# The last 50 microseconds of a Fourier mixer beside softmax attention: eight weight loads earlier on SyncE, two VectorE instructions further back, and two small jobs given to VectorE

## The chip, the cores and the metric

One core of a Trainium2 chip runs the whole program. The metric is device time in microseconds (us), of one execution from start to end. Three runs of the kernel before gave a median of 1685.47 us (1683.25 to 1685.73).

## The reference

Two mixers read the same 2048 x 512 input `x`, and a gate per row blends them:

```python
a = einsum("bsd,ed->bse", x, dft_hid_re); b = einsum("bsd,ed->bse", x, dft_hid_im)
y = einsum("ts,bse->bte", dft_seq_re, a) - einsum("ts,bse->bte", dft_seq_im, b)
...
qkv = x @ wqkv                                   # 32 heads of 16 columns
p = softmax(q @ k.T * 16 ** -0.5)                # 2048 x 2048 for each head
attn = (p @ v) @ wo
...
g = sigmoid((x * gate_w).sum(-1))
out = g * y + (1 - g) * attn
```

## The kernel before

**Tiles.** TensorE (PE) multiplies in fp32r, and where precision matters a value is split in a rounded part "hi" and a rest "lo" (`hi_lo`, line 84: hi by ScalarE, lo by VectorE; `parts`, line 574: both by VectorE). A product is then hi x hi + hi x lo + lo x hi, three matmuls into one PSUM bank. PSUM has eight banks of 128 x 512; a small planner (`bank`, line 384) hands them out in the order in which it believes they come free.

**Heads and units.** The heads run in 16 pairs. The work of a pair is cut into 32 units, 512 in all; a unit is four score tiles (matmul L738, exponential on ScalarE L739 into a tile `pt`). A tile of row maxima is a matmul L223 and a reduction on VectorE (DVE) L225. The values of two units are one group of 16 matmuls in the profile (L774, for the last pair L755).

**Sections.** The program is a written-out stream of sections. A section holds eight score tiles and, mixed in between, other matmuls: first the Fourier part, and near the end the output projection (`proj`, L429: matmuls of attention output by `wo_hl`, three or nine for a row tile of 128 rows). At a section's end come, in this order, the steps of a table `plan` that are due (`at(u, step)`: the step is issued at the end of the section whose first unit is u or u - 1), then a function of its own for some sections (`after`, line 992), then the values of two units. Each engine executes its instructions in the order in which they were issued.

**The last block.** Attention output is stored to HBM, divided by its softmax sums there, and read back as the stationary operand of `proj`. For the last heads of the first 1024 rows this goes as follows. SyncE (SP) stores `osum` (L792) and reads the sums into `rc` (L528, unit 498). DVE takes reciprocals (L534, unit 500), SP stores them to `r` (L539) and loads outputs and reciprocals into `o_raw` (L552, L553: `last_block` step 0). GpSimd (POOL) multiplies the two (L587, step 1, unit 503). DVE rounds the product into `o_l`, hi by L575 and lo by L576 (step 2, unit 505). The `proj` matmuls that read `o_l` begin with the section behind it.

**The last pair.** The last pair's 1024 late rows are done in two blocks of eight units and without HBM (`LastPair`): `copy` moves the sums of the values out of PSUM (L666), `turn` brings them to rows on PE (L672), takes reciprocals (L674) and scales (L676), `back` transposes on PE (L682) and splits into `o15` (L85, L86), and `products` multiplies by `w15` (L691). For block 0 these steps hang between the sections of units 502 to 511, for block 1 they come after the last section (`last_pair`, line 701). `w15` is a rearranged piece of `wo` that eight DMAs load (`load_w15`, L649, unit 504) into the memory that `osum` held.

**The row tiles.** `finish` (line 602) adds a projected tile to the output rows `yp`: either in one DVE instruction (L609), or, for the tiles in `by_others`, by ScalarE (ACT) into `few` (L606) and POOL (L607). Then SP stores the rows (L627, L697).

## Time and profile before

| what | value |
|---|---|
| median of three runs | 1685.47 us |
| the profiled execution: its own time, its span | 1684.99 us, 1683.2 us |
| PE busy, its granted clock | 99% of the span, 0.999 |
| DVE, ACT, POOL busy | 82%, 74%, 45% |
| PE in the chain that ended last | 97% |
| DVE, POOL, DMA in that chain | 1% each |

The span runs from the first instruction to the last; 1.8 us lie around it. PE is busy nearly all the time, so time can only be lost or won where PE stands still, or behind its last matmul. All that the change touches lies in the last 50 us of the span.

### The profile page before, as it was taken

The page shows a single profiled execution, that of the slowest core. Times are in us where ns is not written, and L with a number is a line of the kernel's source. Part 1 is how long each engine was busy: PE and PEld are TensorE (multiplying, and loading weights), DVE is VectorE, ACT ScalarE, POOL GpSimd, SP SyncE. Part 2 cuts the span into 40 slices and gives each one's busy share as a digit, 9 for nine tenths or more (in the row PEclk, how much of TensorE's full clock was granted, in tenths as well). Part 3 has the DMA queues.
Part 4 walks back from the last instruction along what each step waited for, and adds up shares of the span by engine and source line. Part 5 has one row for each costly group of instructions (what it writes and reads, how often), then busy time and mean ns, then how long its engine had stood idle before and what let it go on. Part 6 is the DMA issues. An engine that isn't in the chain of part 4 may idle for free.

```text
span 1683.2 us, 34607 instructions
## 1 busy us (share of the span) xinstructions
PE 1670.9 (99%) x13120; PEld 1014.2 (60%) x13120; DVE 1376.7 (82%) x2295; ACT 1246.9 (74%) x2471; POOL 751.0 (45%) x814
## 2 busy tenths in 40 slices
PE   9999999999999999999999999999999999999997
PEld 7888766655555555555555555555555555555554
DVE  5448688888888888888888888888888888888875
ACT  5212288887777888778777787777777888888885
POOL 0214634544444466445444566454544455422241
PEclk9999999999999999999999999999999999999999
DMA  9973500314141432414165533423241535730114
GB/s 289 344 156 107 177 13 14 52 46 82 45 83 46 88 103 84 77 46 92 39 141 190 103 117 83 93 58 70 70 87 41 103 102 125 275 66 15 34 27 139
DMA packets 82622, 165.16 MB, mean 98 GB/s; under 512 B 19904, under 2 KB 20168, under 8 KB 78616
## 3 DMA queue, kind: packets, MB, share of 16 engines
q1 hardware_dynamic: 77832, 162.30, 37.4%
q8 instruction: 103, 1.69, 0.5%
q0 software_dynamic: 4480, 0.39, 0.3%
q14 instruction: 63, 0.52, 0.1%
q10 hardware_dynamic: 144, 0.26, 0.0%
HBM read 107.73 MB, written 54.52 MB: 96 GB/s over the span
## 4 chain that ended last, share of the span: by engine, by line
PE 97%; DVE 1%; POOL 1%; DMA 1%; issue 0%; SPq 0%; ACT 0%; DVEq 0%; POOLq 0%; ACTq 0%
PE d L429 39%; PE t L774 27%; PE t L223 11%; PE t L738 7%; PE t L318 4%; PE t L89 2%; PE t L90 2%; PE t L91 2%; PE t L336 1%; PE t L755 1%; PE t L429 0%; DVE mx L225 0%; DMA o_raw<-r 0%; PE t L160 0%; POOL hl L295 0%
## 5 line engine op out<-in xcount | busy, mean ns | idle before, releaser
L225 DVE TENSOR_REDUCE mx<-t 128x1 f32<-128x512 f32 x2022 | 1255.5, 684 | 211.1 <-PE t L223 160.4
L739 ACT ACTIVATE pt<-t 128x512 f32<-128x512 f32 x2048 | 1034.5, 629 | 12.4 <-PE t L738 12.2
L738 PE MATMUL t<-qs,ks 50*128 50x512 f32 x2048 | 741.3, 409 | 3.1 <-DVE on L676 2.3
L223 PE MATMUL t<-ks,qs 48*128 48x512 f32 x2022 | 690.1, 400 | 0.1
L429 PE MATMUL d<-xab,ch 64*128 64x512 f32 x2016 | 657.5, 401 | 0.0
L774 PE MATMUL t<-pt,vt 128*32 128x512 f32 x3968 | 477.2, 598 | 0.2
L429 PEld LDWEIGHTS d<-xab,ch 64*128 64x128 f32 x2016 | 357.8, 184 | 130.9 <-issue 98.9
L223 PEld LDWEIGHTS t<-ks,qs 48*128 48x128 f32 x2022 | 367.7, 185 | 82.5 <-ACT pt L739 41.1
L738 PEld LDWEIGHTS t<-qs,ks 50*128 50x128 f32 x2048 | 370.4, 185 | 72.9 <-DVE mx L225 38.6
L429 PE MATMUL d<-xab,cl 64*128 64x512 f32 x1008 | 403.4, 400 | 0.0
L789 POOL TENSOR_TENSOR osum<-osum,oe 128x512 f32<-128x512 f32 x217 | 279.4, 1287 | 161.6 <-ACT oe L783 159.0
L783 ACT COPY oe<-t 128x512 f32<-128x512 f32 x217 | 127.5, 588 | 231.3 <-PE t L774 229.2
L774 PEld LDWEIGHTS t<-pt,vt 128*32 128x32 f32 x3968 | 103.9, 109 | 231.2 <-issue 148.4
L374 POOL CAST ch<-craw 128x512 fp32r<-128x512 f32 x126 | 77.2, 612 | 351.5 <-PE t L738 281.1
L429 PEld LDWEIGHTS d<-xab,cl 64*128 64x128 f32 x1008 | 185.8, 184 | 67.4 <-issue 50.3
L375 POOL TENSOR_TENSOR cl<-craw,ch 128x512 fp32r<-128x512 f32 x126 | 162.3, 1288 | 10.2
L248 POOL DMA_DIRECT2D qs<-mt x132 | 74.1, 567 | 78.8 <-DVE mt L244 73.8
L429 PE MATMUL d<-wo_hl,o_hl 64*128 64x512 f32 x288 | 77.3, 395 | 0.0
L429 PE MATMUL d<-wre,xab 64*128 64x512 f32 x288 | 70.5, 389 | 0.0
L429 PEld LDWEIGHTS d<-wo_hl,o_hl 64*128 64x128 f32 x288 | 52.2, 185 | 13.6 <-DVE yp L609 5.0
L429 PEld LDWEIGHTS d<-wre,xab 64*128 64x128 f32 x288 | 52.9, 185 | 3.8 <-DVE mx L225 0.3
L89 PE MATMUL t<-xab,wh 128*128 128x512 f32 x128 | 50.4, 394 | 0.0
(121 smaller groups left out, 914.0 us busy)
## 6 DMA issues: line engine op xcount, KB each, us to landing
craw<-w_seq SPq DMA_DIRECT2D x128, 256.0 KB
qk<-hl SPq DMA_DIRECT2D x32, 512.0 KB
qs<-qk SPq DMA_DIRECT2D x96, 128.0 KB
ks<-qk SPq DMA_DIRECT2D x96, 128.0 KB
b<-hl SPq DMA_DIRECT2D x16, 512.0 KB
xab<-b SPq DMA_DIRECT2D x16, 512.0 KB
o<-osum SPq DMA_DIRECT2D x62, 128.0 KB
oh<-nh SPq DMA_DIRECT2D x12, 512.0 KB
```

The source lines that it names most:

```text
L89: nc.tensor.matmul(ps, sh, mh, start=first, stop=False)
L223: nc.tensor.matmul(ps, qs[p % 2][r, qt * P:(qt + 1) * P], ks[p % 2][r, kb * 512:(kb + 1) * 512], start=True, stop=True)
L225: user = nc.vector.tensor_reduce(mx[p % 2][:, h, qt, kb:kb + 1], ps, AX.X, ALU.max)
L248: (nc.sync, nc.gpsimd)[h].dma_start(rows.rearrange("v (q b c) -> v b q c", q=n, b=4)[:, b], mt[k % 2][32 * b + h:32 * b + 4 * n:2])
L374: nc.gpsimd.tensor_copy(h1, raw)
L375: nc.gpsimd.tensor_tensor(l1, raw, h1.bitcast(F32), ALU.subtract)
L429: i = nc.tensor.matmul(self.ps, st[r], mv[r], start=not self.begun, stop=stop)
L738: nc.tensor.matmul(ps, ks[p % 2][rr, kt * P:(kt + 1) * P], qs[p % 2][rr, q0:q0 + 512], start=True, stop=True)
L739: return nc.scalar.activation(pts[u][:, 2 * qb + h], ps, AF.Exp, bias=0.0, scale=DH ** -0.5)
L774: nc.tensor.matmul(acc[32 * j:32 * j + 32], vt[:, kt, p, h:h + 32], pt[:, j], start=u == us[0], stop=u == us[-1])
L783: nc.scalar.copy(oe, acc)
L789: nc.gpsimd.tensor_tensor(o, o, oe, ALU.add)
```

## The change

```diff
@@ LastPair.back
-            hi_lo(self.o15[:, 0], self.o15[:, 1], t[:, :P])
+            if self.blk:
+                parts(self.o15[:, 0], self.o15[:, 1], t[:, :P])
+            else:
+                hi_lo(self.o15[:, 0], self.o15[:, 1], t[:, :P])
@@ last_pair
-        by_others.update((5, 6))
+        by_others.add(6)
@@ the plan
-    for step, u in enumerate((500, 503, 505)):
+    for step, u in enumerate((500, 503, 507)):
         at(u, last_block, step, 0, 4, nc.gpsimd)
-    at(504, load_w15)
+    at(499, load_w15)
```

Lines behind 683 stand three lines further down in the kernel of the change (L738 is L741 there, L649 stays).

**The rounding.** On DVE, at the end of the sections of units 504 and 506; the number behind a name is a buffer's. Before:

```order
L609 SCALAR_TENSOR_TENSOR yp15_20723<-d_23280,omg_166,yp15_20723 128x512
L575 CAST o_l_23304<-o_raw_22715 128x1024
L576 TENSOR_TENSOR o_l_23304<-o_raw_22715,o_l_23304 128x1024
L674 RECIPROCAL rc15_23075<-t_23307 128x8
L676 TENSOR_TENSOR on15_23074<-t_23307,rc15_23075 128x4x16 x2
L609 SCALAR_TENSOR_TENSOR yp13_20658<-t_23328,omg_166,yp13_20658 128x512
L609 SCALAR_TENSOR_TENSOR yp14_20722<-t_23342,omg_166,yp14_20722 128x512
L609 SCALAR_TENSOR_TENSOR yp15_20723<-d_23354,omg_166,yp15_20723 128x512
L86 TENSOR_TENSOR o15_23076<-t_23369,o15_23076 128x128
```

And now:

```order
L609 SCALAR_TENSOR_TENSOR yp15_20723<-d_23289,omg_166,yp15_20723 128x512
L674 RECIPROCAL rc15_23075<-t_23304 128x8
L676 TENSOR_TENSOR on15_23074<-t_23304,rc15_23075 128x4x16 x2
L609 SCALAR_TENSOR_TENSOR yp13_20658<-t_23325,omg_166,yp13_20658 128x512
L609 SCALAR_TENSOR_TENSOR yp14_20722<-t_23339,omg_166,yp14_20722 128x512
L609 SCALAR_TENSOR_TENSOR yp15_20723<-d_23351,omg_166,yp15_20723 128x512
L575 CAST o_l_23366<-o_raw_22715 128x1024
L576 TENSOR_TENSOR o_l_23366<-o_raw_22715,o_l_23366 128x1024
L86 TENSOR_TENSOR o15_23076<-t_23369,o15_23076 128x128
```

The two instructions that write `o_l` stood ahead of block 0's reciprocals and now stand one section later, behind three row tiles and ahead of block 0's `o15`.

**The loads.** On SP, from the last store of `osum` on. Before:

```order
L792 DMA o_104<-osum 64x512 x2
L528 DMA rc<-o_104 64x1x64 x2
L248 DMA qs_935<-mt_174 2x4x32 x4
L539 DMA r_151<-rc 16x4x64 x2
L552 DMA o_raw<-o_104 64x1x1024
L553 DMA o_raw<-r_151 64x1x1024
L552 DMA o_raw<-o_104 64x1x1024
L553 DMA o_raw<-r_151 64x1x1024
L649 DMA w_23295<-wo_141 16x1024 x8
L627 DMA out<-yp_21644 128x512
```

And now:

```order
L795 DMA o_104<-osum 64x512 x2
L528 DMA rc<-o_104 64x1x64 x2
L649 DMA w_23127<-wo_141 16x1024 x8
L248 DMA qs_935<-mt_174 2x4x32 x4
L539 DMA r_151<-rc 16x4x64 x2
L552 DMA o_raw<-o_104 64x1x1024
L553 DMA o_raw<-r_151 64x1x1024
L552 DMA o_raw<-o_104 64x1x1024
L553 DMA o_raw<-r_151 64x1x1024
L627 DMA out<-yp_21644 128x512
```

The eight loads of `w15` stood last and now pass the rows of maxima that the scores of the last eight units need (`qs<-mt`), the store of the reciprocals and the four loads of `o_raw`.

**The end.** On DVE, the row tiles 4, 5 and 7 with block 1 of the last pair between them. Before:

```order
L609 SCALAR_TENSOR_TENSOR yp_qs0_22513<-t_23485,omg_166,yp_qs0_22513 128x512
L674 RECIPROCAL rc15_23318<-t_23511 128x8
L676 TENSOR_TENSOR on15_23317<-t_23511,rc15_23318 128x4x16 x2
L86 TENSOR_TENSOR o15_23319<-t_23526,o15_23319 128x128
L609 SCALAR_TENSOR_TENSOR yp_qs0_22513<-t_23530,omg_166,yp_qs0_22513 128x512
```

And now:

```order
L609 SCALAR_TENSOR_TENSOR yp_qs0_22513<-t_23485,omg_166,yp_qs0_22513 128x512
L609 SCALAR_TENSOR_TENSOR yp_qs0_22513<-t_23504,omg_166,yp_qs0_22513 128x512
L674 RECIPROCAL rc15_23315<-t_23510 128x8
L676 TENSOR_TENSOR on15_23314<-t_23510,rc15_23315 128x4x16 x2
L575 CAST o15_23316<-t_23525 128x128
L576 TENSOR_TENSOR o15_23316<-t_23525,o15_23316 128x128
L609 SCALAR_TENSOR_TENSOR yp_qs0_22513<-t_23529,omg_166,yp_qs0_22513 128x512
```

Row tile 5 is one more L609 on DVE and one L606 and one L607 fewer on ACT and POOL; block 1's hi, L85 on ACT before, is L575 on DVE. PE's instructions stand in the same order before and now.

## The prediction

> **What bounds the kernel now.** PE is busy for 99% of the span, so I looked first for the place in the last 55 us where it is not. The waits of PE there name a single one (us in total, times, longest):

> ```profile
> PE t L738 <- DVE on L676: 2.3, 1, 2.3
> ```

> The chain of work that ended last, in order of time, shows how DVE came to be late (start, duration, what):

> ```profile
> 1652.44 2.38 POOL o_raw L587
> ...
> 1654.85 0.70 DVE o_l L575
> ...
> 1655.58 1.23 DVE o_l L576
> ...
> 1656.95 0.37 DVE on L676 x2
> ...
> 1657.45 0.47 PE t L738
> ```

> The reader is to see a detour. PE needs the PSUM bank that L676 reads, so it waits for L676. But L676 has nothing to do with `o_raw`: it stands in DVE's queue behind L575 and L576, and these wait for POOL's product. The timeline of DVE gives its last work ahead of that wait, and the first and the last of the three row tiles behind L676:

> ```profile
> 1651.13 0.75 DVE L609 SCALAR_TENSOR_TENSOR yp<-d,omg,yp 128x512 f32<-128x512 f32 x1
> 1657.22 0.74 DVE L609 SCALAR_TENSOR_TENSOR yp<-t,omg,yp 128x512 f32<-128x512 f32 x1
> 1658.92 0.75 DVE L609 SCALAR_TENSOR_TENSOR yp<-d,omg,yp 128x512 f32<-128x512 f32 x1
> ```

> The timeline of PE gives an undisturbed section (from 1648.73 to L672), the disturbed one (from 1653.98 to the transpose L682) and the first reader of `o_l`:

> ```profile
> 1648.73 0.50 PE L738 MATMUL t<-qs,ks 50*128 50x512 f32 x1
> 1651.10 1.10 PE L672 MATMUL t<-pairsum,oe 128*128 128x64 f32 x8
> 1653.98 0.50 PE L429 MATMUL t<-wo_hl,o_lnh 64*128 64x512 f32 x1
> 1654.56 0.39 PE L429 MATMUL t<-wo_hl,o_lnh 64*128 64x512 f32 x1
> 1654.79 0.39 PE L429 MATMUL t<-wo_hl,o_lnh 64*128 64x512 f32 x1
> 1657.45 0.47 PE L738 MATMUL t<-qs,ks 50*128 50x512 f32 x1 [2.27 <-DVE on L676]
> 1659.04 0.33 PE L682 MATMUL t<-ident,on 128*128 128x128 f32 x1
> 1661.15 0.49 PE L429 MATMUL t<-wo_hl,o_l 64*128 64x512 f32 x1
> ```

> **The rounding moved back.** The sums that the reciprocals read are finished when L672 ends, at 1651.10 + 1.10 = 1652.20; DVE has been idle since 1651.13 + 0.75 = 1651.88. With L575 and L576 gone from its front, the reciprocal and L676 run at once. Between the end of L576 (1655.58 + 1.23 = 1656.81) and that of L676 (1656.95 + 0.37 = 1657.32) lie 0.5, so they end near 1652.8. PE's matmuls follow each other at 0.23 (1654.79 - 1654.56), so it asks for the bank at 1655.02, when it has been free for 2.2. The matmul of 1657.45 runs **2.43 earlier**.

> What is late next? First the transpose L682, which waited for row tiles. The undisturbed section took 2.37 from its first matmul to L672 (1651.10 - 1648.73); from 1653.98 that makes 1656.35. The second row tile of the section reads the two L429 behind the bank, which start at 1655.0 to 1655.3 and end by 1655.7; with its 0.75, one such tile ahead of it on DVE, it is through at 1656.5. So the transpose comes at 1656.5 to 1656.7 where it was at 1659.04: the gain is still 2.3 to 2.5. Then `o_l`, which now stands behind the third row tile. That tile ended at 1658.92 + 0.75 = 1659.67 and moves with PE to 1657.25. L575 adds 0.70, L576 1.23, the gaps 0.05: hi at 1658.0, lo at 1659.25. The first reader of hi moves from 1661.15 to about 1658.7. The third matmul of that row tile, the first reader of lo, stands 0.58 behind (1654.56 - 1653.98), at 1659.3. So hi has 0.7 of slack and lo hardly any; I take no wait, and keep up to 0.5 of loss for the range. POOL's product, ready at 1654.82, has 2.4 to spare. `o15` of block 0 (L86) now follows L576; its reader, L691, comes a full section later.

> The term: **-2.4 us** (-1.9 to -2.6).

> **The eight loads moved forward.** SP's DMA queue in the timeline (start, duration of the group):

> ```profile
> 1634.84 1.21 SPq L528 DMA_DIRECT2D rc<-o  x2
> 1639.78 2.73 SPq L248 DMA_DIRECT2D qs<-mt  x4
> 1643.55 1.21 SPq L539 DMA_DIRECT2D r<-rc  x2
> 1647.34 5.26 SPq L649 DMA_DIRECT2D w<-wo  x8
> ```

> And what SP waited for:

> ```profile
> SPq L248 <- DVE mt L244: 3.6, 1, 3.6
> SPq L649 <- DMA o_raw<-r: 1.3, 1, 1.3
> SPq L649 <- DMA o_raw<-o: 0.5, 1, 0.5
> ```

> The 5.26 hold 1.8 of waiting for loads of `o_raw` that stood ahead; without it the eight take 3.46, 0.43 each. The neighbours L528 and L539 take 0.6 each (1.21 for two), the dearest that I would assume: 4.8 for eight. In the new place they start at 1634.84 + 1.21 = 1636.05 behind transfers that are small or done, and end at 1639.5 to 1640.9. SP stood idle there for 3.6, waiting for the row maxima, so `qs<-mt` moves by 0 to 1.1. Who waits for it? The fifth score of a section, in the timeline of PE:

> ```profile
> 1645.47 0.49 PE L738 MATMUL t<-qs,ks 50*128 50x512 f32 x1
> ```

> The only landing that the trace gives for these transfers is that of POOL's four:

> ```profile
> DMA to landing us min/median/max: 1.6/1.7/3.4
> ```

> The last of SP's four went out a quarter of 2.73 ahead of the group's end, at 1641.8, and landed by that near 1643.5: 2.0 ahead of its reader, 0.3 at the longest landing. A shift of 1.1 leaves 0.9, or costs 0.8; I take 0, since 0.43 is this very transfer's price. The store of the reciprocals keeps its time, as it waits for DVE until 1643.55. The loads of `o_raw` lose their company and may land sooner; once the rounding has moved, nobody waits for that. Term: **0** (0 to +0.8).

> [...]

> **The end of the program.** Tile 5's matmuls are the first row of PE's timeline here; tile 7's are the third, and the last is the product with `o15`:

> ```profile
> 1672.18 0.98 PE L429 MATMUL t<-wo_hl,o_l 128*128 128x512 f32 x3
> 1674.69 0.33 PE L682 MATMUL t<-ident,on 128*128 128x128 f32 x1
> 1674.78 0.94 PE L429 MATMUL t<-wo_hl,o_l 128*128 128x512 f32 x3
> 1675.69 0.97 PE L691 MATMUL t<-w,o 32*128 32x512 f32 x12
> ```

> DVE ahead of the reciprocal, and ACT:

> ```profile
> 1674.04 0.21 DVE L674 RECIPROCAL rc<-t 128x8 f32<-128x8 f32 x1 [1.37 <-PE t L672]
> ```

> ```profile
> 1674.79 0.69 ACT L606 ACTIVATE few<-d,omg 128x512 f32<-128x512 f32 x1 [0.85 <-PE d L429]
> 1675.37 0.26 ACT L85 CAST o<-t 128x128 fp32r<-128x128 f32 x1
> ```

> Tile 5 is ready for DVE at 1672.18 + 0.98 = 1673.16, and DVE is idle for 1.37 ahead of the reciprocal; an L609 (0.74) ends at 1673.9, before 1674.04: free. Block 1's hi waited on ACT behind tile 6. Rounding 128 x 128 from PSUM on DVE is not in the trace; between a reciprocal of 8 columns (0.21) and a row tile of 512 (0.74), I take 0.26, what ACT needs. The transpose ends at 1675.02, so hi is there at 1675.35 instead of 1675.63. But PE has tile 7 to do until the third matmul has started near 1675.33, so L691 starts at 1675.56 at best, 0.13 sooner. Does the end follow? The DMA engines in windows (last columns: busy share, GB/s):

> ```profile
> 1677.00:1677.40 0.40, 0.00 (x0) 1.00 0.00 0
> 1677.40:1681.60 4.20, 1.27 (x1) 0.86 0.97 373
> ```

> 4.2 us at 373 GB/s are 1.57 MB, the last six stored tiles (tiles 6, 7 and block 1's four, 128 x 512 x 4 bytes each), without a gap. The train starts with tile 6, which keeps its way over ACT and POOL. Tile 5 was out of its way before, since the engines stood at 0 ahead of it. Term: **0** (-0.4, if the end follows the chain instead, to +0.1).

> **Sum.** -2.4 against the profiled execution's 1684.99 is 1682.6 (span 1680.8). That execution lies 0.48 below the median of the runs; from the median it is 1683.1, which I give: 0.14% less.

> **The rivals.**
> - *The wait becomes one for `o_l`.* If the row tiles run later than drawn, PE waits at the first reader of lo, one for one. For it: lo has no slack. Against it: hi has 0.7 and POOL 2.4. With a whole L576 lost, 1.2: 1684.3.
> - *The loads hold up SP: slower.* If they wait in the new place as two of them did in the old, they push `qs<-mt`. The gain is gone when that shift reaches 2.0 + 2.4 = 4.4, that is when the eight take 3.6 + 4.4 = 8.0, or 1.0 each. At 1.2 each the shift is 6.0 and the score waits 4.0: 1685.47 - 2.4 + 4.0 = 1687.1. Against it: what they waited for then is not ahead of them now. [...]
> - *The bank was not what PE waited for.* The releaser is inferred. If it was another, nothing is won: 1685.4. Against it: L676 ended at 1657.32, and PE started 0.13 later.
> - *More than forecast.* The end follows the chain by 0.4: -2.8, 1682.7.

> **How the numbers follow.** Forecast 0.68, `o_l` 0.12, SP 0.08 (half of it slower than before), bank 0.04, more 0.08. A measurement of this kernel can tell about 0.2%, 3.4 us, from no change, and no case reaches that by itself on the fast side. But the three runs lie 2.5 us apart, so a median can be a microsecond off: a fifth of the forecast and half of "more" fall beyond, 0.18. Slower: half of the SP case and a little of the bank, 0.06. Within: 0.76. The range takes the forecast with "more" and the scatter below it (1680.9), and `o_l` and the bank above (1685.7).

> **What would show it.** Right: no L676 in the waits of PE; the L575 of `o_l` directly behind an L609 and not behind POOL; the first matmul of `o_l` 2.3 to 2.5 sooner, counted from the first of the section before; `qs<-mt` no later than 1.1 behind its old distance from L244. Wrong: a wait of PE for L576, or for a DMA at the fifth score behind L248; a train of stores that starts over 0.3 sooner behind the last values.

## The result and the profile after

The changed kernel takes **1681.95 us** (median of 20 executions, 1681.30 to 1682.79), the kernel before beside it 1685.50 (20 executions, 1683.25 to 1688.00). The ratio is 0.9981, with a 95% interval of 0.9975 to 0.9987: 0.19% less, 3.2 to 3.6 us. Two things are to be explained. The gain is about 1 us larger than the forecast, and the executions of the kernel before lie 4.75 us apart, those of the changed one 1.5. Between the two profiled executions the gain is only 1684.99 - 1682.39 = 2.60.

The waits of PE in the last 55 us of the changed kernel are an empty list. The timeline of PE has the section that was disturbed before (start, duration; from L429 at 1653.80 to the transpose L682) and the first matmuls that read `o_l`:

```profile
1650.91 1.10 PE L672 MATMUL t<-pairsum,oe 128*128 128x64 f32 x8
...
1653.80 0.50 PE L429 MATMUL t<-wo_hl,o_lnh 64*128 64x512 f32 x1
...
1654.38 0.62 PE L741 MATMUL t<-qs,ks 50*128 50x512 f32 x2
...
1656.42 0.33 PE L682 MATMUL t<-ident,on 128*128 128x128 f32 x1
1656.68 1.92 PE L758 MATMUL t<-pt,vt 128*32 128x512 f32 x16
1658.54 0.49 PE L429 MATMUL t<-wo_hl,o_l 64*128 64x512 f32 x1
...
1659.11 0.39 PE L429 MATMUL t<-wo_hl,o_l 64*128 64x512 f32 x1
```

From the section's first matmul to the first reader of `o_l` it took 7.17 before (1661.15 - 1653.98) and takes 4.74 now: 2.43 less. The rest of the 2.60 between the profiles is 0.18 that lay upstream of the section already (1653.98 against 1653.80). DVE in the same stretch:

```profile
1652.05 0.21 DVE L674 RECIPROCAL rc<-t 128x8 f32<-128x8 f32 x1 [0.35 <-PE t L672]
1652.29 0.36 DVE L676 TENSOR_TENSOR on<-t,rc 128x64 f32<-128x64 f32 x2
1654.80 1.45 DVE L609 SCALAR_TENSOR_TENSOR yp<-t,omg,yp 128x512 f32<-128x512 f32 x2 [2.15 <-PE t L429]
1656.31 0.75 DVE L609 SCALAR_TENSOR_TENSOR yp<-d,omg,yp 128x512 f32<-128x512 f32 x1
1656.98 0.68 DVE L575 CAST o_l<-o_raw 128x1024 fp32r<-128x1024 f32 x1
1657.69 1.22 DVE L576 TENSOR_TENSOR o_l<-o_raw,o_l 128x1024 fp32r<-128x1024 f32 x1
```

The reader is to see three things. The reciprocal waits for PE alone. L676 is through at 1652.65, so the bank is free long before PE asks for it (1654.61, the second of the two scores from 1654.38). And L576 ends at 1658.91, 0.20 ahead of its first reader at 1659.11. SP's queue and POOL's product:

```profile
1634.66 1.21 SPq L528 DMA_DIRECT2D rc<-o  x2
1635.92 3.83 SPq L649 DMA_DIRECT2D w<-wo  x8
1639.85 2.74 SPq L248 DMA_DIRECT2D qs<-mt  x4
```

```profile
1651.74 2.37 POOL L587 TENSOR_TENSOR o_raw<-o_raw 128x1024 f32<-128x1024 f32 x1 [9.67 <-DMA o_raw<-r]
```

The eight loads take 0.48 each and fill what was SP's wait for the row maxima. The fifth score starts 1.19 behind its section's first matmul, as before (1645.29 - 1644.10; 1645.47 - 1644.28). POOL's product starts 0.5 sooner beside the upstream 0.18; whether that is because the loads of `o_raw` have no weights beside them is not shown (see the eight loads alone). The end, from PE, from DVE (block 1's hi) and in windows around the train of the last stores (last two columns: DMA share, GB/s):

```profile
1673.02 0.97 PE L694 MATMUL t<-w,o 32*128 32x512 f32 x12
```

```profile
1672.43 0.29 DVE L575 CAST o<-t 128x128 fp32r<-128x128 f32 x1 [0.42 <-PE t L682]
```

```profile
1674.70:1675.10 0.40, 0.00 (x0) 0.00 (x0) 0.40 (x2) 0.00 (x0) 0.32 (x1) 1.00 0.00 0
1675.10:1679.00 3.90, 0.00 (x0) 0.00 (x0) 1.01 (x2) 0.00 (x0) 0.94 (x1) 0.71 1.04 402
```

From the last product to the end of the span it is 7.58 (1680.6 - 1673.02), before 7.51 (1683.2 - 1675.69). The end has given nothing.

### The profile page after: what moved, and what is told of

Its sections match the earlier page's. It is cut to its first block, busy times and chain, and to the rows that moved or that the text cites. A ratio compares the mean times of both kernels' runs of the same rounds, so it can differ in the third digit from the quotient of the medians.

```text
span 1680.6 us, 34603 instructions
## 1 busy us (share of the span) xinstructions
PE 1670.8 (99%) x13120; PEld 1016.6 (60%) x13120; DVE 1378.1 (82%) x2297; ACT 1245.8 (74%) x2469; POOL 750.9 (45%) x813
## 4 chain that ended last, share of the span: by engine, by line
PE 98%; POOL 1%; DVE 1%; issue 0%; DMA 0%; SPq 0%; ACT 0%; DVEq 0%; POOLq 0%; ACTq 0%
PE d L429 40%; PE t L777 27%; PE t L223 11%; PE t L741 7%; PE t L318 4%; PE t L90 2%; PE t L89 2%; PE t L91 2%; PE t L336 1%; PE t L758 1%; PE t L429 1%; DVE mx L225 0%; PE d L223 0%; PE t L160 0%; POOL hl L295 0%
## 5 line engine op out<-in xcount | busy, mean ns | idle before, releaser
L741 PE MATMUL t<-qs,ks 50*128 50x512 f32 x2048 | 741.6, 409 | 0.8 <-ACT y L445 0.5
L429 PE MATMUL d<-xab,ch 64*128 64x512 f32 x2016 | 657.5, 401 | 0.0
L429 PEld LDWEIGHTS d<-xab,ch 64*128 64x128 f32 x2016 | 357.7, 184 | 132.9 <-issue 98.9
L741 PEld LDWEIGHTS t<-qs,ks 50*128 50x128 f32 x2048 | 370.4, 185 | 67.1 <-DVE mx L225 37.9
L429 PE MATMUL d<-xab,cl 64*128 64x512 f32 x1008 | 403.6, 400 | 0.0
L429 PEld LDWEIGHTS d<-xab,cl 64*128 64x128 f32 x1008 | 185.7, 184 | 67.8 <-issue 51.1
L248 POOL DMA_DIRECT2D qs<-mt x132 | 74.3, 568 | 77.7 <-DVE mt L244 72.6
L429 PE MATMUL d<-wo_hl,o_hl 64*128 64x512 f32 x288 | 77.3, 395 | 0.0
L429 PE MATMUL d<-wre,xab 64*128 64x512 f32 x288 | 70.4, 389 | 0.0
L429 PEld LDWEIGHTS d<-wo_hl,o_hl 64*128 64x128 f32 x288 | 52.2, 185 | 13.4 <-DVE yp L609 5.0
L429 PEld LDWEIGHTS d<-wre,xab 64*128 64x128 f32 x288 | 52.9, 185 | 3.9 <-DVE mx L225 0.3
```

What stands on the lines that cost most here:

```text
L248: (nc.sync, nc.gpsimd)[h].dma_start(rows.rearrange("v (q b c) -> v b q c", q=n, b=4)[:, b], mt[k % 2][32 * b + h:32 * b + 4 * n:2])
L429: i = nc.tensor.matmul(self.ps, st[r], mv[r], start=not self.begun, stop=stop)
L741: nc.tensor.matmul(ps, ks[p % 2][rr, kt * P:(kt + 1) * P], qs[p % 2][rr, q0:q0 + 512], start=True, stop=True)
```

## The experiments

Four theories stood against each other. **W**: all of the gain is PE's one wait on L676, and that wait is longer or shorter from run to run. **L**: what the medians have beyond it comes from the weights, which no longer load beside `o_raw`. **E**: it comes from the end. **C**, formed after the first four runs: PE's idle time lets its granted clock fall in a part of the executions. Each kernel below ran against the kernel before on the same chip; intervals are 95%.

### The rounding alone

```diff
 kernel before
-    for step, u in enumerate((500, 503, 505)):
+    for step, u in enumerate((500, 503, 507)):
```

> The kernel before with the rounding of the last block one section later and nothing else (507 for 505). Theory W (all of the gain is PE's one wait, and its length varies from run to run with the landing of o_raw, so its mean is larger than the profiled 2.27): the whole gain comes here, a median near 1682.0 and runs that lie within 2 us of each other, as those of the change do; no wait of PE on L676. Theory L (what goes beyond the forecast 2.4 comes from the weights no longer loading beside o_raw): 1683.1 here. Theory E (it comes from the end of the program): 1683.1 here too.

Measured: 1681.63 (1681.29 to 1682.15, 11 runs), ratio 0.9978 (0.9969 to 0.9987). That is the whole gain, and the spread is gone with it. PE waits for nothing in the last 50 us of its profile. L and E fall as causes of the rest.

### The eight loads alone

```diff
 kernel before
-    at(504, load_w15)
+    at(499, load_w15)
```

> The kernel before with the eight weight loads moved forward and nothing else (499 for 504). Theory W: o_raw lands 0.5 to 0.7 sooner than in the profile of before, PE's wait on L676 is still there and shorter by that, 1684.5 to 1685.0, and the runs still spread over 3 us or more. Theory L: about 1684.4, and the spread becomes small, as the weights were what disturbed the landing. Theory E: as before less the 0.5 at most.

Measured: 1685.13 (1683.11 to 1686.70, 11 runs), ratio 0.9996 (0.9987 to 1.0005): no difference. Its profile shows something new. The timeline of PE, and four slices of 0.25 us (third column from the end: the granted clock):

```profile
1655.94 0.47 PE L738 MATMUL t<-qs,ks 50*128 50x512 f32 x1 [1.78 <-DVE on L676]
...
1657.87 3.47 PE L755 MATMUL t<-pt,vt 128*32 128x512 f32 x16
```

```profile
1657.25:1657.50 0.25, 0.12 (x2) 0.00 (x0) 0.25 (x2) 0.25 (x2) 0.00 (x0) 1.00 0.00 0
1657.50:1657.75 0.25, 0.24 (x1) 0.14 (x1) 0.25 (x1) 0.25 (x2) 0.00 (x0) 0.72 0.00 0
...
1660.75:1661.00 0.25, 0.25 (x4) 0.00 (x0) 0.00 (x0) 0.00 (x0) 0.00 (x0) 0.50 0.00 0
1661.00:1661.25 0.25, 0.25 (x4) 0.00 (x0) 0.00 (x0) 0.00 (x0) 0.00 (x0) 0.96 0.00 0
```

The wait is 0.5 shorter than before (1.78), since POOL's product comes sooner: 0.86 behind the start of L672 (1650.93 - 1650.07) against 1.34 before (1652.44 - 1651.10). That the new place of the loads does this is not shown, as the product comes just as soon, 0.88 behind (1650.56 - 1649.68), in the kernel with PE kept busy, where the loads stand in their old place. But 1.7 us after PE is back at work its clock goes to a half, and stays there for 3.4 us. The 16 value matmuls take 3.47 where they took 1.92: 1.55 lost, behind the wait. That the wait is the cause is theory C, which comes from this run.

### The end alone

```diff
 kernel before
-            hi_lo(self.o15[:, 0], self.o15[:, 1], t[:, :P])
+            if self.blk:
+                parts(self.o15[:, 0], self.o15[:, 1], t[:, :P])
+            else:
+                hi_lo(self.o15[:, 0], self.o15[:, 1], t[:, :P])
...
-        by_others.update((5, 6))
+        by_others.add(6)
```

> The kernel before with the two edits at the end and nothing else (both parts of block 1's rounding and tile 5 on VectorE). Theory W and L: nothing, within 0.2 of before (1685.3 to 1685.7), with the spread of before; the train of stores at the end starts at the same distance behind the last value group. Theory E: 1684.4, and the train starts about 1 us sooner.

Measured: 1685.37 (1683.37 to 1687.21, 11 runs), ratio 0.9999 (0.9990 to 1.0008). These edits are worth nothing, and the spread is that of before.

### Tile 6 on DVE as well

```diff
 changed kernel
-        by_others.add(6)
```

> The kernel of the change with row tile 6 on VectorE too, so that only block 1's first tile still goes over ScalarE and GpSimd. If the end is a train of six stores that starts with tile 6 (as the prediction has it), the train starts 1 to 1.3 us sooner and the end comes 0.3 to 0.7 sooner: 1681.3 to 1681.6. If the end follows VectorE's chain, tile 6's 0.75 stands ahead of block 1's rounding and the end comes 0.3 to 0.5 later: 1682.3 to 1682.5.

Measured: 1681.31 (1680.80 to 1681.98, 11 runs), ratio 0.9979 (0.9970 to 0.9988), 0.3 below the rounding alone on the same chip. The ratios (0.9979 and 0.9978) do not tell the two apart, so the step rests on the medians and on the profile:

```profile
1673.18 0.97 PE L694 MATMUL t<-w,o 32*128 32x512 f32 x12
```

Its span is 1680.2, so the end comes 7.0 behind the last product, against 7.5 to 7.6 in the three kernels in which tile 6 goes over ACT and POOL (7.51 before, 7.58 changed, 7.63 with the end alone: 1682.1 - 1674.47). That fits a train of stores which starts with tile 6, and not an end that follows VectorE's chain, which would have come later.

### PE kept busy during the wait

```diff
 kernel before, in the section of unit 506, ahead of the score that waits
+            if valued == 506 and n == 4:
+                dum = d_bank()
+                for _ in range(9):
+                    nc.tensor.matmul(dum, wos[0][:, 0, 0, :P], wos[0][:, 0, 1], start=True, stop=True)
             if not ahead and slot != "d":
                 score(slot[0], 1 - half)
```

> The kernel before, with nine matmuls of 128x512 into the PSUM bank of the d chain (0.23 us each, 2.05 us; their result is never read) put on PE directly ahead of the score that waits for the bank of L676. The bank comes free as late as before, so PE is at work during most of the 2.3 us in which it stood idle, and the score starts no sooner. Theory C (clock: PE's idle of 1.8 to 2.4 us lets the granted clock fall to a half for some 3.4 us in a part of the executions, about 1.5 us each time): the falls go, median 1683.8 (1683.2 to 1684.3), all runs within 1.5 us of each other, no slice of the clock below 0.9. Theory W (the length of the wait itself differs from run to run, with the landing of o_raw): nothing changes, median near 1685.2, runs 3 to 4 us apart.

Measured: **1683.90 (1683.45 to 1684.54, 11 runs)**, before 1685.17 (1683.28 to 1687.53, 32 runs); ratio 0.9993 (0.9984 to 1.0001). PE is given matmuls that nobody needs, and the kernel gets 1.3 us faster in the medians. The ratio's interval just touches 1; the spread says it more clearly, with 1.1 us between 11 runs against 4.25 between 32. The timeline of PE:

```profile
1653.69 2.33 PE L950 MATMUL d<-wo_hl 128*128 128x512 f32 x9
...
1657.53 0.33 PE L682 MATMUL t<-ident,on 128*128 128x128 f32 x1 [0.15 <-DVE yp L609]
1657.79 1.92 PE L755 MATMUL t<-pt,vt 128*32 128x512 f32 x16
```

The transpose comes as late behind L672 as before (7.85 against 7.94), so the wait is still paid, in dummies. The granted clock of this profile is 1.00 in its slices from 1648 to 1666 and from 1668 to 1678, past the last matmul. W expected 1685.2 and falls; C has its number.

### Four dummies in place of nine

```diff
-                for _ in range(9):
+                for _ in range(4):
```

> As the run before, with four matmuls in place of nine, so that about 1.35 us of PE's idle stay. Theory W: median near 1685.2, runs 3 to 4 us apart, as before. Theory C says only that it lies between: 1683.8 and close runs if an idle of 1.35 us is too short to let the clock fall, up to 1685.2 and wide runs if it is long enough.

Measured: 1683.74 (1683.26 to 1685.53, 11 runs), ratio 0.9989 (0.9980 to 0.9998). Eight runs lie at 1683.3 to 1684.0, three at 1685.1 to 1685.5, and nothing between. The profiled execution is one of the three (1685.53):

```profile
1656.28 0.46 PE L738 MATMUL t<-qs,ks 50*128 50x512 f32 x1 [1.18 <-DVE on L676]
...
1658.11 3.62 PE L755 MATMUL t<-pt,vt 128*32 128x512 f32 x16
```

```profile
1658.25:1661.50 3.25, 3.25 (x16) 0.48 (x12) 0.54 (x2) 1.24 (x4) 0.00 (x0) 0.50 0.02 5
```

The clock fell behind an idle of 1.18 us too, but in fewer executions: three of eleven by their times. (The three are told by their times: the one at 1685.06 has a mean clock of 0.999, the other two 0.998.)

### An idle put into the changed kernel

```diff
 changed kernel, behind L676
+            if not self.blk:
+                other = work.tile([P, 4, 2, DH], F32, name="on_b")
+                for _ in range(3):
+                    nc.sync.dma_start(other, self.on)
+                    self.on, other = other, self.on
```

> The changed kernel, with the result of L676 of block 0 sent three times through a DMA between two SBUF tiles ahead of the transpose L682 (about 2 us each), so that PE stands idle at the transpose for some 2.5 us, with o_raw, the weights and the roundings where the change put them. Theory C: the wait is paid and on top of it the clock falls in a part of the runs: median 1682 + 2.5 + 0.5 to 1.5 = 1685.0 to 1686.0, runs 3 to 4 us apart. Theory W: only the wait is paid, 1684.5, and the runs stay within 2 us of each other, since o_raw stands ahead of nothing that PE waits for.

Measured: 1683.49 (1682.80 to 1685.55, 11 runs), ratio 0.9991 (0.9982 to 1.0000). Half a miss: the spread of 2.75 lies between W's 2 and C's 3 to 4, and the median lies 1.5 below what C expected. Of that, 0.7 is the wait, which was 1.84 and not 2.5: the three DMAs follow each other on SP at 1.87 and 1.85 (1651.42, 1653.29, 1655.14). The rest is that the median holds no fall: 1683.49 is 1.85 above the kernel with sixteen loads on the same chip, that is the wait alone. Six executions lie at 1682.8 to 1683.5 and five at 1684.2 to 1685.6. In the profiled one (1682.81) the clock did not fall:

```profile
1657.06 0.30 PE L687 MATMUL t<-ident,on_b 128*128 128x128 f32 x1 [1.84 <-DMA on_b<-on]
1657.29 1.92 PE L763 MATMUL t<-pt,vt 128*32 128x512 f32 x16
```

### The same, longer

```diff
-                for _ in range(3):
+                for _ in range(5):
```

> The changed kernel, with the result of L676 of block 0 sent five times through a DMA between two SBUF tiles ahead of the transpose L682, where e10_idle sent it three times. A pass took 1.9 us there and PE waited 1.84, so it should wait 5.6 to 5.7 us here: longer than any distance from PE's last work to the fall of the clock in the profiles so far (1.9 to 4.9 us at the ends of the programs). Theory C: the clock falls in every execution, the profile shows it at a half when PE starts again, and up to 3.4 us of work run at half speed: 1687.6 for the wait alone and 0.8 to 1.7 on top, 1688.4 to 1689.3. Without the clock's part the time is 1686.7 (by the fast half of the runs of e10_idle, 3.8 more) to 1687.6.

Measured: **1688.77 (1688.26 to 1689.75, 11 runs)**, ratio 1.0019 (1.0010 to 1.0028). PE in the timeline and the clock in windows of 2 us:

```profile
1660.52 0.45 PE L687 MATMUL t<-ident,on_b 128*128 128x128 f32 x1 [5.47 <-DMA on_b<-on]
1660.90 3.44 PE L763 MATMUL t<-pt,vt 128*32 128x512 f32 x16
```

```profile
1656.00:1658.00 2.00, 0.00 (x0) 0.00 (x0) 1.45 (x2) 0.95 (x2) 0.00 (x0) 0.79 0.15 45
1658.00:1660.00 2.00, 0.00 (x0) 0.00 (x0) 0.00 (x0) 0.00 (x0) 0.00 (x0) 0.50 0.18 53
1660.00:1662.00 2.00, 1.48 (x9) 0.58 (x13) 0.29 (x1) 0.27 (x1) 0.00 (x0) 0.50 0.04 9
1662.00:1664.00 2.00, 2.00 (x12) 0.20 (x4) 0.00 (x0) 0.00 (x0) 0.00 (x0) 0.50 0.00 0
1664.00:1666.00 2.00, 2.00 (x17) 1.26 (x13) 0.74 (x2) 1.17 (x3) 0.00 (x0) 1.00 0.00 0
```

No `o_raw`, no weights and no rounding stand behind this wait, and the clock falls: here in every execution, as all eleven have a mean clock of 0.996 or 0.997. The 1688.77 is what C gave, 1.2 to 2.1 above the wait alone.

### Sixteen loads of half the size

```diff
 changed kernel
-        for i in range(8):
-            nc.sync.dma_start(w[16 * i:16 * i + 16].bitcast(F32), wo_d[3][64 * (i % 2) + 3:64 * (i % 2) + 64:4])
+        for i in range(16):
+            r0 = 64 * (i // 2 % 2) + 32 * (i % 2)
+            nc.sync.dma_start(w[8 * i:8 * i + 8].bitcast(F32), wo_d[3][r0 + 3:r0 + 32:4])
```

> The changed kernel with the weights of w in 16 loads of half the size at the new place, the SP rival of the prediction with its price forced up. At 0.48 us each they hold SP for 7.7 us in place of 3.8, so qs<-mt on SP goes out some 3.7 us later. With the slack of 2.0 us that the prediction worked out, the fifth score waits 1.7 us: 1683.7 by theory W, up to 1684.9 by theory C, if that idle lets the clock fall as well. If the slack were nothing, 3.7 us: 1685.7; if qs<-mt has over 3.7 us, or an issue of half the size costs half as much, no wait: 1682.0.

Measured: 1681.64 (1681.21 to 1682.37, 10 runs), ratio 0.9977 (0.9968 to 0.9987): no wait. SP's queue, and how long the four `qs<-mt` that POOL issues in this stretch took to land:

```profile
1634.94 5.57 SPq L650 DMA_DIRECT2D w<-wo  x16
1640.62 2.75 SPq L248 DMA_DIRECT2D qs<-mt  x4
```

```profile
DMA to landing us min/median/max: 2.4/2.7/3.2
```

A load of half the size costs 0.35 and not 0.48, so the row maxima are held up by less than 3.7. SP's four started 0.27 ahead of POOL's four before (1640.05 - 1639.78), and start 1.75 behind them here (POOL's at 1638.87): a shift of 2.0, and the time does not move. The fifth score stands 1.40 behind its section's first matmul (1644.49 - 1643.09), where it stood 1.19; two scores later nothing of that is left (2.02 in both). That fits a slack near 2.0 that is just used up, though no row names what held the score.

### The kernel before, with both tiles on DVE and the rounding moved

```diff
 kernel before
-        by_others.update((5, 6))
...
-    for step, u in enumerate((500, 503, 505)):
+    for step, u in enumerate((500, 503, 507)):
```

> The kernel before, with the rounding moved back to (500, 503, 507) and tiles 5 and 6 of the last block finished on DVE in place of ACT and POOL; the eight loads of the weights stay at 504 and the last rounding stays on ACT and DVE. If the gain is the wait and the clock alone, and tile 6 on DVE starts the train of the last stores sooner, this is the fastest version: 1681.0 (1680.5 to 1681.6), as the run with tile 6 on DVE gave 0.6 less than the changed kernel and the run with the rounding alone 0.3 less. If either of the two pieces left out matters (loads forward, parts on DVE), it is above 1681.7.

Measured: 1681.41 (1680.87 to 1681.78, 11 runs), ratio 0.9975 (0.9966 to 0.9984); the end of the span comes 7.0 behind the last product (1679.8 - 1672.78). It beats the kernel before, and by its median the changed one too, by 0.5, without the other two pieces; the intervals of the two ratios overlap, so that second step rests on the 0.5 at the end of the span. Between it and the changed kernel with tile 6 on DVE (1681.31) nothing can be told.

### The kernel before, twice more

The edit is empty lines.

> The kernel before itself, with empty lines in its source and nothing else, for one more profile of it. Theory C: if this execution takes 1685.0 us or more, its profile shows PE's wait on L676 of 1.8 to 2.4 us and then the granted clock at a half for 3.4 us (once; for 1686.7 or more for twice that), with the 16 matmuls of L755 or their neighbours slowed by as much; if it takes less than 1684.6, the wait alone. Theory W: in a long execution the wait itself is longer, 3.5 us or more, and the clock stays at 1.00.

> As the run before, once more, since four in ten executions of the kernel before show no fall of the clock in their mean. Theory C: at 1685.0 us or more a wait of 1.8 to 2.4 us and a fall of 3.4 us or twice that; below 1684.6 the wait alone. Theory W: a longer wait and no fall.

Measured: 1686.69 and 1685.48, one execution each. Both profiles show a wait of ordinary length (2.27 in the profile of before, 2.37 with the end alone) and a fall of the clock behind it. The first, from the timeline of PE and in windows of 3 us:

```profile
1657.52 0.47 PE L741 MATMUL t<-qs,ks 50*128 50x512 f32 x1 [2.48 <-DVE on L676]
...
1659.36 3.45 PE L758 MATMUL t<-pt,vt 128*32 128x512 f32 x16
```

```profile
1657.00:1660.00 3.00, 2.32 (x16) 1.25 (x19) 2.46 (x5) 1.97 (x5) 0.00 (x0) 0.94 0.00 0
1660.00:1663.00 3.00, 3.00 (x18) 0.70 (x12) 0.29 (x1) 0.74 (x3) 0.00 (x0) 0.50 0.02 5
```

And the second:

```profile
1656.65 0.47 PE L742 MATMUL t<-qs,ks 50*128 50x512 f32 x1 [2.39 <-DVE on L676]
```

```profile
1657.00:1660.00 3.00, 3.00 (x19) 1.38 (x19) 1.76 (x4) 2.72 (x6) 0.00 (x0) 0.54 0.02 5
1660.00:1663.00 3.00, 3.00 (x28) 1.35 (x20) 0.54 (x2) 0.78 (x2) 0.00 (x0) 0.89 0.00 0
```

W expected a wait of 3.5 or more in a long execution and finds 2.4 and 2.5. In the two profiles the clock is 1.00 in 367 and 368 slices of 4 us up to 1624, and from 1654 to 1670 it is below 0.99 in the fall alone. Behind the last matmul, while only stores run, it falls as well: at 1680.46 in the profile of before, whose last matmuls end at 1676.66, and at 1676.74 in that of the changed kernel, with the end at 1673.99. There PE has nothing left to lose. The first lies at the very limit from which C expected two falls (1686.7), and its profile has one.

## Why the prediction was right, and where it was too small

The time lies in the range (1680.9 to 1685.7), 1.15 below the forecast of 1683.1, and the gain of 0.19% lies at the edge of "within 0.2%". It lies below every case that was drawn (the lowest, "more than forecast", was 1682.7): what keeps it in the range is the microsecond that was allowed there for scatter, which is luck.

**The rounding moved back: right.** The bank was what PE waited for, L676 ends at 1652.65 (1652.8 was drawn), the transpose comes 2.62 behind its section's first matmul (2.5 to 2.7 drawn), and `o_l` is read 2.43 sooner (2.3 to 2.5). `hi` has 0.88 of slack and `lo` 0.20, as the working had it: hardly any, and no wait. The rival of a wait for `o_l` is missed by 0.2 us. The rounding alone gives all of the gain. One step came out by luck: the score that waited runs 2.66 sooner, not 2.43 (1657.45 - 1653.98 before, 1654.61 - 1653.80 now). Scores run beside the L429, not behind them (the section's first L429 and first score both start at 1653.80), so PE had asked for the bank 0.23 ahead of the 1655.02 that was drawn. The scores behind it follow more slowly now, and the transpose gains 2.44. The term holds by the second way of working it, over the transpose and the row tiles.

**The eight loads: right.** They take 3.83 (3.46 to 4.8), the row maxima shift by 0.26 (0 to 1.1), no score waits. With sixteen loads the shift is 2.0 and still nothing is lost, so the rival that ends slower was far off: it needed 4.4. Whether weights on their way hold up the row maxima behind them in SP's queue is not shown, as the landing of SP's own four is in no trace. POOL's four, in another queue, took 2.7 (median) with the sixteen loads, 1.8 with the eight and 1.7 before. What made the 2.7 is not shown, and it cost nothing here.

**The end: right.** It follows the train of stores. Block 1's hi took 0.29 on DVE against 0.26 estimated; the end alone changed nothing, and only tile 6 moves it, by 0.5. The rival "more than forecast" comes nearer to the time (1682.7), but for a wrong reason: it wanted the end to follow the chain by 0.4.

**What was too small** is the term "-2.4 us", and the step behind it is the sentence that "the three runs lie 2.5 us apart, so a median can be a microsecond off". The scatter was taken for error of measurement, so the sum of one profile was carried over to the median unchanged. It was an effect of the very wait that the change removes: the eleven executions with the rounding alone, where the wait is gone, lie 0.86 apart, those with the end alone, where it stands, 3.84. In the 86 executions of the kernel before beside the first ten experiments, by their mean clock:

| mean granted clock | executions | median, us |
|---|---|---|
| 0.999 | 34 | 1684.1 |
| 0.998 | 39 | 1685.45 |
| 0.997 | 13 | 1687.3 |

A fall of 3.4 us to a half takes 1.7 us of clock, 0.001 of 1681. The mean also holds the fall behind the last matmul, which costs no time, and it is rounded, so the groups overlap: 0.999 goes from 1683.20 to 1686.30, 0.998 from 1684.74 to 1687.46. The profiled execution of before had no fall at the wait, and its sum is exact for an execution without one (windows of 2 us; third column from the end: the granted clock):

```profile
1656.00:1658.00 2.00, 0.55 (x5) 0.55 (x6) 1.93 (x5) 0.17 (x2) 0.00 (x0) 1.00 0.00 0
1658.00:1660.00 2.00, 1.85 (x17) 0.85 (x17) 1.45 (x2) 2.00 (x5) 0.00 (x0) 1.00 0.04 8
1660.00:1662.00 2.00, 2.00 (x20) 0.85 (x14) 0.29 (x1) 0.95 (x4) 0.00 (x0) 1.00 0.00 0
```

The two parts, by three kernels on one chip: from 1685.17 to 1683.90 with PE kept busy is 1.27 for the falls, and from there to 1681.64, in the kernel with sixteen loads that has no wait, 2.26 for the wait. The 2.26 are the term; the 1.27 were missing.

What decides whether the clock falls **stays open**. The length of the idle alone does not: it fell after 1.18 in one profile and not after 1.84 in another, nor after 2.27 and 2.37. The slices show how long a fall lasted: 3.41 us with the loads alone (1657.61 to 1661.02; a slice from 1657.50 with a mean of 0.72 is at full clock for 0.11), 3.42 with four dummies (1658.19 to 1661.61) and 6.83, twice that, with the long idle (1657.17 to 1664.00). With the loads alone the clock falls again behind the last matmul, at 1681.50:

```profile
1681.25:1681.50 0.25, 0.00 (x0) 0.00 (x0) 0.00 (x0) 0.00 (x0) 0.00 (x0) 1.00 1.04 393
1681.50:1681.75 0.25, 0.00 (x0) 0.00 (x0) 0.00 (x0) 0.00 (x0) 0.00 (x0) 0.50 0.89 336
```

That is 23.89 us behind the start of the first, and with four dummies it is 23.90 (1658.19 to 1682.09). What sets the moment of a fall, and in which executions it falls, is not shown by any run. For the executions of before at 0.997 no profile was taken, and that they hold two falls is an inference from their mean.

## What to carry to other kernels

An idle stretch of the engine that bounds the kernel can cost more than its length: here the clock fell up to 4.6 us after PE had stopped, and the 16 value matmuls then took up to 3.62 us in place of 1.92. Look at the granted clock in the 5 us behind such a stretch, and take the spread of the runs for a trace of something that happens in some of them, before taking it for error. A sum made from one profile holds for executions like that one; compare its mean clock with those of the other runs before carrying it to a median. Here useless matmuls in the place of the wait already won back the clock's part (1.27 us of the median); where a wait can't be removed, that is worth a try.
